# Two more tiles turned on TensorE and six more gate buffers in a recurrence-and-router kernel

## The chip, the cores and the metric

One core of one Trainium2 chip runs the whole kernel. The metric is device time in microseconds (us) from launch to end. TensorE (PE), VectorE (DVE), ScalarE (ACT), GpSimd (POOL) and SyncE (SP) each run their own instructions in order, and meet only at semaphores. SP, ACT and POOL can also issue DMAs, which move data between the chip's memory (HBM) and the on-chip buffers (SBUF).

## The reference, cut to what matters

```python
# x, f_logit: (4, 5056, 256); B*S = 20224 tokens, D = 256, E = 8 experts, F = 1024
f = lb + (1 - lb) * sigmoid(f_logit)
h[t] = f[t] * h[t-1] + (1 - f[t]) * x[t]            # per batch and channel; y[t] = h[t]
logits = normalise(y) @ normalise(emb).T / tau      # 20224 x 8
e = argmax(logits);  g = softmax(logits)[e]
out[token] = g * (relu(y[token] @ w1[e]) @ w2[e])   # one expert per token
```

## The kernel before, in words

**First half: chunks.** The tokens are taken in 40 chunks of 512 (the last has 256). For each chunk SP loads `f_logit` and `x` (`load`, three buffers each). PE transposes them so that channels lie on partitions (`F_`, `X_`), ACT makes the forget gate (L791, L797), and DVE does the recurrence as a scan along the tokens (L838). `Y_` turns the result back to token rows, in bf16, in `Yt`: early chunks by PE, from chunk 14 on by a transposing DMA that SP issues (L869). `route_` and `gate_` find each token's expert, its gate weight and its place in that expert's list. POOL then scatters each 128 rows into the HBM scratch `Xs` with an indirect DMA (L1107). A row of `Xs` is 256 bf16 values, the gate weight and the token's number: the "token and gate words" of the change.

**Second half: tiles.** As soon as an expert's list has 256 rows, they can be a tile. `update_` writes a small table that says for each tile where its rows start in `Xs` and which expert's weights it needs. `tile_(j, u, g, n)` emits tile `j` as the `n`-th in order. Its steps are:

- Load of the rows into `ys` as two 128 x 256 halves, channels on partitions. For all but the first tiles this is a transposing DMA on SP (`ld`, L1329). For the first `NPE` = 4 tiles SP issues a plain load into the output buffer `osb` instead (`ldp`, L1350), PE multiplies its four 128 x 128 blocks by the identity (`turn`, L1381), and ACT copies the result into `ys` (L1395).
- Load of the gate weight and token number of each row into `xm[n % NX]`, `NX` = 8 (`ldm`, L1339). SP issues it for 75 tiles. The six main tiles of the last table (`last`, j = 75 to 80, taken in order places n = 70, 72, 74, 76, 78 and 80) come in halves, and there ACT issues the `xm` loads.
- `mm1` on PE (L1432, 16 matmuls of 256 columns, or 32 of 128 for the last table's tiles), relu into `hT` by ACT (L1453) and DVE (L1458), `mm2` on PE (L1480, 16 matmuls).
- Scaling by the gate into `osb[n % 6]`, one half by ACT (L1495) and one by DVE (L1499). Both read `xm`.
- Two indirect DMAs on POOL that scatter 128 rows each to `out` (L1505). They read `osb`, and take the token numbers from `xm`.

So an `xm` buffer is free again only when both scatters of the tile that used it have landed: the load of tile n waits for the scatters of tile n - `NX`. In the same way `osb` is reused after 6 tiles, and `ys` after 6 (there it is `mm1` that must have read it).

**The order of the work.** A planner (`Prog.schedule`) decides before launch the order in which each engine issues its instructions. It simulates the engines with costs written in the code, and takes at each moment the ready operation of lowest priority number: chunk work first, tiles after. An operation is ready in it when the operations that it depends on have ended by its own clock. The order of each queue is then fixed, and `emit` puts in front of each instruction the waits that correctness needs. If something lands later on the chip than in the plan, its engine stands there, and everything behind it in that queue stands too. Output scatters and `Xs` scatters also wait for a step of PE that lies ahead of them in the plan (`paced`). PSUM has eight banks, which are given out in the plan by kind (`Hold`: "a" for chunk work and turns, "m" for `mm1`, "o" for `mm2`).

The lines that set the loads and their buffers:

```python
qx, qy, qh, qo = n % NX, n % NYS, n % NHT, n % NO        # L1318
op("act" if last else "sp", lambda e, s=s: ldm(e, s), ..., r=rd, w=[("xm", qx, k) ...], order=[lo])  # L1367
```

Of the kernel before, what the change touches and what calls it, by code (L numbers as in the profile page):

```python
# [370 lines left out]
def bass_hgrn_recurrence__then__cosine_router_kernel(  # L371
# [41 lines left out]
    with ExitStack() as es:  # L413

        def sb(name, shape, dt=F32):
            return es.enter_context(nc.sbuf_tensor(name, shape, dt))
# [70 lines left out]
        nullv = sb("nullv", [P, 2])  # L487
        tbl = [sb(f"tbl{q}", [P, 2], I32) for q in range(NU)]
        nrow = sb("nrow", [P, E], I32)
        NX = 8  # L490
        xm = [sb(f"xm{q}", [P, 2, 2], I32) for q in range(NX)]
        NHF = 3
        hbf = [sb(f"hbf{q}", [P, DT * CH], BF16) for q in range(NHF)]
        CT = 14
        NYS = 6
        NPE = 4
        ys = [sb(f"ys{q}", [P, T * DT], BF16) for q in range(NYS)]
        NHT = 2
        hT = [sb(f"hT{q}", [P, FT, T], BF16) for q in range(NHT)]
# [816 lines left out]
        def tile_(j, u, g, n):  # L1316

            qx, qy, qh, qo = n % NX, n % NYS, n % NHT, n % NO  # L1318
            last = u == len(ups) - 1
# [5 lines left out]
            def ld(e, s):  # L1325
                r = reg(e, f"row{j}_{s}")
                e.load(r, tbl[u][rows[s] : rows[s] + 1, 0:1])
                r = evl[j, s] = e.snap(r, donate=True, min_val=0, max_val=NULLROW)
                return e.dma_start_transpose(  # L1329
                    ys[qy][:, s * R_ * DT : (s + 1) * R_ * DT].rearrange("p (k t) -> p k t", k=DT),  # L1330
                    Xs[bass.ds(r, R_), 0:P].bitcast(BF16),
                )

            def ldm(e, s):
                if last:
# [5 lines left out]
                    Xs[bass.ds(evl[j, s], R_), P : P + 2].rearrange(  # L1341
                        "(p s) r -> p s r" if j < NPE else "(s p) r -> p s r", p=P
                    ),
# [15 lines left out]
            for s in range(halves):  # L1359
                lo = op(  # L1360
                    "sp", ldp, 950, r=rd, w=[("osb", qo, k) for k in range(2)],
                    dma=f"xs{qy}", nbytes=140000,
                ) if j < NPE else op(
                    "sp", lambda e, s=s: ld(e, s), 1750, r=rd, w=[("ys", qy, k) for k in ([s] if last else [0, 1])], dma=f"xs{qy}" + "b" * s,
# [8 lines left out]

            if j < NPE:
                hy = Hold("a")
# [255 lines left out]
```

## Time and profile before

| | us |
|---|---|
| median of three timed runs | 472.71 (471.99 to 473.21) |
| the profiled execution | 476.37 |
| its span, from the first to the last instruction | 474.6 |
| PE busy | 438.5 (92%) |
| DVE, ACT, POOL busy | 359.6, 325.6, 332.0 |
| DMA | 100.47 MB, mean 212 GB/s |

Durations of single instructions come from the profiled execution. A group of matmuls is shown as one line with its first start and its length; as they are pipelined, the distance between the starts of two groups says what a group costs PE. "Idle before" is how long an engine had stood ahead of an instruction, with the event that ended it. "issue" there means that nothing shown ended it. DMA-issuing instructions are not in the busy time of SP and ACT; POOL's indirect DMAs are, with 0.30 us of issue between any two.

### The profile page before, as it was taken

To read this page: it belongs to the slowest core of one execution; us is meant where nothing else is said; L and a number is where in the kernel's file an instruction comes from. 1 tells how busy PE (TensorE), PEld (TensorE's weight loads), DVE (VectorE), ACT (ScalarE), POOL (GpSimd) and SP (SyncE) were. 2 spreads that over 40 slices of the span, in tenths; PEclk is the share of its full clock that TensorE was granted. 3 is DMA by queue.
4 is the path that set the end of the run, shared out by engine and by line. 5 is a ranking of instruction groups with operands and counts; after the bars stand their busy time and mean duration, and the time that the engine had idled before them with its cause. 6 is when DMAs were issued, how large, how long until landed. Compare 5 with 4: busy or idle time off the path is not lost. (4 is left out here: it accounts for less than half of the span.)

```text
span 474.6 us, 12386 instructions
## 1 busy us (share of the span) xinstructions
PE 438.5 (92%) x4098; PEld 376.5 (79%) x4098; DVE 359.6 (76%) x1075; ACT 325.6 (69%) x571; POOL 332.0 (70%) x388
## 2 busy tenths in 40 slices
PE   6866868889989999999999999999999999979994
PEld 4564555669768889888888789999999999969993
DVE  6887999999998999999999997545545455345442
ACT  4877898999899899899899555444444444244441
POOL 8144657767776777777777777777777777775554
PEclk8989999999999999999999999999999999989999
DMA  7999999999999999999996644655454444553311
GB/s 235 309 308 309 309 320 324 293 286 263 279 269 301 301 305 304 313 312 283 256 287 159 142 110 133 144 136 133 120 133 131 127 109 116 150 137 101 94 62 68
DMA packets 120481, 100.47 MB, mean 212 GB/s; under 512 B 97940, under 2 KB 99487, under 8 KB 120416
## 3 DMA queue, kind: packets, MB, share of 16 engines
q1 hardware_dynamic: 102464, 59.37, 47.9%
q0 software_dynamic: 16224, 40.26, 31.3%
q8 instruction: 36, 0.59, 0.5%
q10 hardware_dynamic: 1728, 0.01, 0.2%
q14 instruction: 29, 0.24, 0.2%
HBM read 58.93 MB, written 32.93 MB: 194 GB/s over the span
## 5 line engine op out<-in xcount | busy, mean ns | idle before, releaser
L1505 POOL DMA_INDIRECT out_dram<-osb,xm x162 | 160.7, 992 | 63.2 <-issue 30.2
L1107 POOL DMA_INDIRECT XsScratch<-Yt,sli x158 | 152.3, 964 | 57.9 <-issue 25.9
L1432 PE MATMUL bank<-ys,wall 128*128 128x256 bf16 (+1 forms) x1392 | 161.5, 267 | 3.4 <-ACT hT L1453 2.8
L1480 PE MATMUL bank<-wall,hT 128*128 x1296 | 161.3, 273 | 0.2 <-issue 0.2
L1432 PEld LDWEIGHTS bank<-ys,wall 128*128 x1392 | 146.7, 145 | 7.3 <-ACT hT L1453 3.3
L1480 PEld LDWEIGHTS bank<-wall,hT 128*128 128x128 bf16 x1296 | 125.3, 98 | 19.6 <-issue 2.2
L1453 ACT ACTIVATE hT<-bank 128x512 bf16<-128x512 f32 x162 | 96.2, 596 | 38.6 <-PE bank L1432 37.0
L1458 DVE TENSOR_SCALAR hT<-bank 128x512 bf16<-128x512 f32 x162 | 110.7, 684 | 12.5 <-PE bank L1432 7.4
L1499 DVE TENSOR_SCALAR osb<-bank,xm 128x256 f32<-128x256 f32 x81 | 38.9, 480 | 83.2 <-ACT osb L1495 81.7
L838 DVE TENSOR_TENSOR_SCAN hb<-fg,hb,bank 128x512 f32<-128x512 f32 (+4 forms) x78 | 95.9, 1235 | 0.1
L1495 ACT ACTIVATE osb<-bank,xm 128x256 f32<-128x256 f32 x81 | 38.5, 476 | 71.7 <-PE bank L1480 58.0
L797 ACT ACTIVATE fg<-th,cs 128x512 f32<-128x512 f32 (+1 forms) x80 | 64.1, 814 | 2.0 <-DVE cs L625 1.0
L814 PE MATMUL bank<-ident,xin 128*128 128x128 f32 x316 | 50.0, 283 | 12.7 <-ACT fg L797 10.7
L822 DVE SCALAR_TENSOR_TENSOR bank<-fg,bank 128x512 f32<-128x512 f32 (+1 forms) x80 | 54.4, 685 | 3.4 <-PE bank L814 2.8
L814 PEld LDWEIGHTS bank<-ident,xin 128*128 128x128 f32 x316 | 36.2, 144 | 22.0 <-ACT fg L797 14.2
L791 ACT ACTIVATE th<-bank 128x512 f32<-128x512 f32 (+1 forms) x80 | 46.1, 592 | 10.8 <-PE bank L780 10.6
L780 PE MATMUL bank<-ident,fin 128*128 128x128 f32 x316 | 47.7, 279 | 3.2 <-DMA fin<-in_f_logit_dram 1.2
L780 PEld LDWEIGHTS bank<-ident,fin 128*128 128x128 f32 x316 | 37.3, 144 | 7.9 <-issue 1.7
L850 ACT ACTIVATE sq<-hb 128x1024 f32<-128x1024 f32 (+1 forms) x40 | 41.9, 1048 | 1.7 <-DVE hb L838 1.5
L943 PE MATMUL bank<-hb,eT 128*8 128x512 f32 (+1 forms) x160 | 40.8, 588 | 0.0
L947 PE MATMUL bank<-sq,onesf 128*1 128x512 f32 (+1 forms) x160 | 40.7, 586 | 0.0
L859 ACT ACTIVATE hbf<-hb 128x512 bf16<-128x512 f32 x50 | 31.3, 632 | 3.5 <-DVE hb L838 2.0
(139 smaller groups left out, 298.1 us busy)
## 6 DMA issues: line engine op xcount, KB each, us to landing
fin<-in_f_logit_dram SPq DMA_DIRECT2D x39, 512.0 KB
xin<-in_x_dram SPq DMA_DIRECT2D x39, 512.0 KB
wall<-in_moe_w_dram POOLq DMA_DIRECT2D x16, 512.0 KB, 10.4
out_dram<-osb,xm POOLq DMA_INDIRECT x162
XsScratch<-Yt,sli POOLq DMA_INDIRECT x158
ys<-XsScratch SPq DMA_TRANSPOSE x83, 2.8
xm<-XsScratch SPq DMA_DIRECT2D x75, 2.0 KB
osb<-XsScratch SPq DMA_DIRECT2D x4, 136.0 KB
```

The lines of the kernel that those rows point to most:

```text
L780: i = e.transpose(bank[h.b][:, b : nb * P : nb], fin[q][:, b, dh * P : (dh + 1) * P], ident[:],)
L791: lambda e, dh=dh, h=h: e.activation(th[dh][:, 0:n], bank[h.b][:, 0:n], AF.Tanh, scale=0.5),
L797: lambda e, dh=dh: e.activation(fg[c % 2][:, dh, 0:n], th[dh][:, 0:n], AF.Identity, bias=cs[:, dh, 0:1], scale=cs[:, dh, 1:2],),
L814: i = e.transpose(bank[h.b][:, b : nb * P : nb], xin[q][:, b, dh * P : (dh + 1) * P], ident[:],)
L822: lambda e, dh=dh, h=h: e.scalar_tensor_tensor(out=bank[h.b][:, 0:n], in0=fg[c % 2][:, dh, 0:n], scalar=1.0, in1=bank[h.b][:, 0:n], op0=AL ...
L838: lambda e, dh=dh, s0=s0, s1=s1, init=init, h=h: e.tensor_tensor_scan(hb[c % NH][:, dh, s0:s1], fg[c % 2][:, dh, s0:s1], bank[h.b][:, s0:s ...
L1107: lambda e, j=o + j, i=o + k_ * 4 + b: e.indirect_dma_start(out=Xs[:, :], out_offset=bass.IndirectOffsetOnAxis(ap=sli[y][:, j : j + 1], axis=0
L1432: i = e.matmul(bank[hh[f // 2].b][:, at : at + R_], wall[:, bass.ds(a1[j, s][(4 * mp + f) * DT + kt] - WA - WREV, 2 * FT * P),].bitcast(BF ...
L1453: lambda e, o=o, h=h: e.activation(o, bank[h.b][:], AF.Relu), 512,
L1458: lambda e, o=o, h=h: e.tensor_scalar(o, bank[h.b][:], 0.0, None, op0=ALU.max),
L1480: i = e.matmul(po(s), hT[qh][:, kf, s * P : (s + 1) * P], wall[:, bass.ds(a2[j, s if last else 0][kf] - WA, 2 * D)].bitcast(BF16), start=( ...
L1505: lambda e, s=s: e.indirect_dma_start(out=out[:, :], out_offset=bass.IndirectOffsetOnAxis(ap=xm[qx][:, s, 1:2], axis=0), in_=osb[qo][:, s, :],
```

## The change: two numbers

The tiles j = 0 to 5 now take the plain load, the turn on PE and the ACT copy; before, j = 0 to 3 did. In `ldm` the row order that goes with the plain load holds for them too. The `xm` buffers are 14 instead of 8. Nothing else is edited; the planner makes its order anew from these numbers.

```diff
-        NX = 8
+        NX = 14
         xm = [sb(f"xm{q}", [P, 2, 2], I32) for q in range(NX)]
...
-        NPE = 4
+        NPE = 6
```

## Rows read from the trace of the kernel before

**Rows 1.** The page's parts 1 and 2: busy time; busy tenths in 40 slices.
```profile
PE 438.5 (92%) x4098; PEld 376.5 (79%) x4098; DVE 359.6 (76%) x1075; ACT 325.6 (69%) x571; POOL 332.0 (70%) x388
...
PE   6866868889989999999999999999999999979994
```

**Rows 2.** Windows of 12 us: stretch, length, busy us (count) by engine, clock, DMA.
```profile
84.00:96.00 12.00, 10.04 (x90) 7.30 (x90) 11.59 (x32) 11.97 (x20) 9.56 (x11) 1.00 1.08 304
96.00:108.00 12.00, 11.62 (x119) 9.46 (x120) 10.95 (x42) 11.17 (x22) 7.76 (x9) 1.00 1.14 282
108.00:120.00 12.00, 11.94 (x117) 10.36 (x118) 11.26 (x34) 11.47 (x21) 9.20 (x10) 1.00 1.10 265
120.00:132.00 12.00, 11.56 (x114) 10.05 (x107) 11.37 (x37) 10.08 (x19) 9.25 (x10) 1.00 1.10 286
132.00:144.00 12.00, 10.74 (x94) 8.12 (x92) 11.09 (x30) 11.12 (x20) 8.62 (x10) 1.00 1.25 258
144.00:156.00 12.00, 12.00 (x127) 10.01 (x126) 11.18 (x45) 10.83 (x19) 8.61 (x10) 1.00 1.10 281
...
396.00:408.00 12.00, 12.00 (x112) 11.34 (x111) 5.57 (x10) 5.34 (x11) 9.26 (x10) 1.00 0.44 119
```

**Rows 3.** Windows of 2 us around 418 us, same columns.
```profile
416.00:418.00 2.00, 0.00 (x0) 0.00 (x0) 0.31 (x1) 0.82 (x2) 1.59 (x2) 1.00 0.63 153
418.00:420.00 2.00, 1.80 (x9) 1.42 (x10) 1.74 (x4) 1.48 (x4) 1.39 (x3) 0.50 0.38 109
420.00:422.00 2.00, 2.00 (x14) 1.48 (x13) 0.80 (x2) 0.60 (x1) 1.70 (x2) 0.64 0.75 197
```

**Rows 4.** Timeline of PE, the `mm1` groups there: start, us, instruction, idle before.
```profile
411.08 1.91 PE L1432 MATMUL bank<-ys,wall 128*128 128x256 bf16 x16
...
414.58 1.04 PE L1432 MATMUL bank<-ys,wall 128*128 128x256 bf16 x8
418.20 1.92 PE L1432 MATMUL bank<-ys,wall 128*128 128x256 bf16 x8 [2.59 <-ACT hT L1453]
...
422.41 1.91 PE L1432 MATMUL bank<-ys,wall 128*128 128x256 bf16 x16
```

**Rows 5.** Timeline of ACT and its DMA queue (ACTq) in the same stretch.
```profile
409.54 0.60 ACT L1453 ACTIVATE hT<-bank 128x512 bf16<-128x512 f32 x1 [0.28 <-PE bank L1432]
415.73 1.33 ACTq L1339 DMA_DIRECT2D xm<-XsScratch  x2
417.18 0.47 ACT L1495 ACTIVATE osb<-bank,xm 128x256 f32<-128x256 f32 x1 [7.05 <-issue]
```

**Rows 6.** Timeline of POOL: last scatter to `Xs`; output scatter 37th from the end.
```profile
399.34 0.96 POOL L1107 DMA_INDIRECT XsScratch<-Yt,sli  x1 [0.30 <-PE bank L1432]
...
412.23 0.99 POOL L1505 DMA_INDIRECT out_dram<-osb,xm  x1 [0.30 <-PE bank L1432]
```

**Rows 7.** Waits of SP: engine, line, waited for; us in total, times, longest.
```profile
SPq L348 <- DMA out_dram<-osb,xm: 29.9, 23, 3.1
```

**Rows 8.** Timeline of SP: a plain tile load; first two transposing ones (tiles 4, 5).
```profile
85.09 0.35 SPq L1350 DMA_DIRECT2D osb<-XsScratch  x1
...
95.33 4.27 SPq L1329 DMA_TRANSPOSE ys<-XsScratch  x1
...
101.28 1.74 SPq L1329 DMA_TRANSPOSE ys<-XsScratch  x1
```

**Rows 9.** Timeline of PE: tile 1's turn, what follows, and tile 4's `mm1`.
```profile
96.31 0.40 PE L1381 MATMUL bank<-identb,osb 128*128 128x128 bf16 x4 [1.20 <-DMA osb<-XsScratch]
96.54 0.51 PE L965 MATMUL bank<-ident,lgS 98*128 98x98 f32 x4
...
123.60 1.04 PE L1432 MATMUL bank<-ys,wall 128*128 128x256 bf16 x8
```

**Rows 10.** Waits of PE: the turns' own.
```profile
PE bank L1381 <- DMA osb<-XsScratch: 1.2, 1, 1.2
```

**Rows 11.** Groups by line: ACT's copies of the turned tiles (count, busy us, mean ns).
```profile
L1395 ACT ACTIVATE ys<-bank 128x512 bf16<-128x512 f32 x4 | 2.4, 610 | 0.7 <-PE bank L1381 0.7
```

## The prediction

> **What bounds the kernel now.** I read the page's first two parts, then windows, then the timelines of the places where TensorE (PE) has holes. PE is busy 438.5 of 474.6 us, more than any other engine, and its 40 slices show where the rest lies [rows 1]: the first nine slices (to about 107 us), then 9s, one 7 near 415 us, and the end. The windows sharpen it: PE stands 1.96 us in 84 to 96, and 0.38, 0.06, 0.44 and 1.26 us in the next four windows (12.00 less the busy time), 2.14 together; from 144 us on it has 12.00 of 12.00, and so to 408 us (the first and the last of these windows stand in [rows 2]; one between them lacks 0.48). So PE sets the end: work added to it costs its length unless it falls into one of these holes, and only a closed hole gives time back.
>
> The hole near 415 us is the one that the change touches. Two `mm1` groups start at 411.08 and 414.58, which is 3.50 us for one tile; the next whole one starts at 422.41, 7.83 us after [rows 4]. One tile took 4.33 us too long. Of these 2.59 us are idle PE, put down to ACT's relu [rows 4]. The rest is clock: the granted clock is 1.00, but after 416 to 418, in which PE does nothing, it is 0.50 (1.2 GHz) in one window and 0.64 in the next [rows 3]; at half speed 1.80 busy us cost 0.90, and 0.36 of 2.00 us costs 0.72. With 2.59 that is 4.21, the same to 0.1 us.
>
> ACT is late because it stands in its own queue. It ends a relu at 409.54 + 0.60 = 410.14, and its next instructions are two `xm` loads that go out at 415.73; the gate scaling behind them had waited 7.05 us for nothing shown but "issue" [rows 5]. That 5.59 us is a semaphore wait. Which one? These are the halves of tile j = 75, at place n = 70, the first whose `xm` load ACT issues. With eight buffers it must wait for the scatters of place 62. The last place is 80, two scatters each, so the second scatter of place 62 is the 37th from the end: issued 412.23, done on POOL at 413.22 [rows 6]. ACT's load follows 2.51 us later, what a scatter would need to land. Place 62's rows had been scaled long before: its `mm1` is four tiles, some 14 us, ahead of place 66's at 407.6 (one tile before the row at 411.08). POOL lags PE, and its distance reaches back over eight buffers.
>
> **The change part by part.** *Fourteen `xm` buffers.* The load of place 70 now waits for place 56, six tiles earlier: twelve output scatters, and the last two to `Xs`, which stand between. At 1.29 us each (0.99 and 0.30 of issue [rows 6]) that is 18.1 us, so it has landed near 415.73 - 18.1 = 397.6, before ACT comes to the load at 410.14. The ACT stall of 5.59 us goes, and with it PE's 4.33 us. What is late next? Three things. The same load also needs all rows in `Xs`: the last such scatter ends at 399.34 + 0.96 = 400.30 [rows 6], with 2.51 us to land 402.8. The plan can't put the load much before that, as it comes after the row load of its tile, whose `ys` buffer is freed by the `mm1` of place 64 (two tiles before 411.08, at 404.1). The `osb` buffers, six, would be the next limit: place 68's scaling needs the scatters of place 62, landed at 415.73, and falls without the stall at about 418. That holds with 2 us to spare and more later, since a tile costs POOL 2.58 us and PE 3.50. The third is PE itself, which is full again. I take -4.33; bounds -4.33 and 0.
>
> SP loses its waits for output scatters, 29.9 us in 23 waits [rows 7]. They cost PE nothing now, as it is full while SP stands (these waits lie after 250 us, where its only hole but 0.48 us is this one), so their end gives nothing: 0, on either side.
>
> *Tiles 4 and 5 turned on PE.* Removed: two transposing loads, whose issue holds SP for 4.27 and 1.74 us [rows 8]. Added: two plain loads of 0.35 us each on SP, eight matmuls, two ACT copies. The next PE group begins 0.23 us after a turn [rows 9], so two turns are 0.46 us, in windows that are full but for 2.14 us [rows 2]; I count them whole: +0.46, bounds 0 and +0.80 (two times the 0.40 us length).
>
> The Trainium skill, "TensorE: Matmul & The Clock Gate", Part 4 (PE-mode transpose), gives about 275 ns for one 128 x 128 bf16 transpose inside a kernel. As an estimate by that page the eight would be 2.2 us, and the sum below would be -1.5 instead of -3.3. Here a block is an ordinary matmul against the identity, and the row has four of them in 0.23 us; the row decides.
>
> A turn adds a wait on PE, and behind it stands all of PE's queue: the chunks' transposes, which feed ACT and DVE, and the tiles. Of the four turns now one waited, tile 1's, 1.20 us [rows 9, 10]: its plain load was issued at 85.09 and PE could start at 96.31, 11.2 us after [rows 8, 9], in a stretch where the DMA engines are full (share above 1 in every window [rows 2]). Two more turns: between 0 and 2.40 us; I take the mean of the four, 0.30 each: +0.60.
>
> The two ACT copies are 0.61 us each [rows 11], 1.22 us where ACT is busy 11.17 and 11.47 of 12 [rows 2]. It has 1.36 us free in these two windows, so I take 0; without that cover up to +1.22, as PE's transposes of `x` wait for the gate that ACT makes.
>
> What SP gains, 4.27 + 1.74 - 0.70 = 5.31 us, lets the next chunk loads go out earlier, and a plain load may move through the DMA engines faster than a transposing one. Tile 4's own data is in no hurry: it was asked for at 95.33 and first used at 123.60 [rows 8, 9]. PE's holes there are all that this can give: between 0 and -2.14 [rows 2]. I take 0, since PE's order is fixed and the holes have several causes. The planner makes a new order from the two numbers; that can open or close holes of the size seen in 120 to 144, 0.44 to 1.26 us [rows 2]. I cost it at 0, with 1.3 us either way.
>
> The sum: -4.33 + 0.46 + 0.60 = -3.27. The profiled execution took 476.37 us (span 474.6 and 1.8 around it), so it would be 473.1; the median of the timed runs is 3.66 us lower, and I put the same step on it: 472.71 - 3.27 = 469.4.
>
> **The rivals.** *The hole is mostly the profiler's.* The timed runs are 3.66 us shorter than the profiled one. PE has nothing to give between 144 and 414 us, so the difference comes from the start, the hole or the end. POOL issues scatters without a pause, so if it is slightly quicker in a timed run, place 62's scatter lands in time. If all 3.66 are the hole, only 0.67 is left to win and 1.06 of turns is added: 473.1, no change. For it: the size fits; 320 scatters would make up the 5.59 us at 0.017 us each. Against: the first 107 us hold far more idle time in which an execution can differ. Chance 0.20.
>
> *The wait moves to another event of POOL.* With the buffer free, the plan puts ACT's load earlier, where it waits for the last `Xs` scatter, landing at 402.8, or the scaling waits for `osb`. POOL's lag is the same, and ACT again stands several us. Then 472.71 + 1.06 = 473.8, no change. For it: POOL was 5.59 us later than the plan put it. Against: the row load comes first in the plan, and the 2 us to spare on `osb`. Chance 0.08.
>
> *The turns stall PE, slower.* If the plan puts the two new turns as near to their loads as tile 1's, and these take longer to land in the fuller stretch (1.14 against 1.08 [rows 2]), PE stands in a stretch whose order is fixed. From 3.3 us in the two together the gain of the hole is gone, from 4.7 it is slower by more than can be told. Five us beyond the 0.46, two of tile 1's waits in each turn, give 472.71 - 4.33 + 0.46 + 4.8 = 473.6; the same beside a hole that the timed runs hardly have (0.67) gives 472.71 - 0.67 + 0.46 + 4.8 = 477.3. For it: one of four waited. Against: the other three did not make PE wait, and chunk work fills PE meanwhile. With the planner's new order in a worse shape as its second way to the same end, chance 0.12.
>
> **How the numbers follow.** My forecast, -3.27 with its bounds, has 0.60: 469.4, by itself 466.7 (no waits at the turns, 1.3 from the order, some of the holes) to 471.3. Up to the first two rivals the range reaches 474.0; above it lies most of the slower case, and together with what is below 466.7 I leave out some 0.17. What a measurement can tell from no change is 0.3%, 1.4 us: faster is below 471.3. The forecast case gives 0.58 of that and a hole that is half the profiler's 0.05, so 0.63; the same 0.21; slower 0.16.
>
> **What would show it.** Right: ACT's two `xm` loads near place 70 go out without a gap ahead of them; PE's `mm1` groups stay 3.50 us apart through 405 to 425 us, with the clock at 1.00; six turns of about 0.23 us, the waits for plain loads under 2.4 us together; windows full from 144 us on as before. Wrong: an ACT gap of several us in the same place with another scatter landing at its end; a new PE hole behind a turn between 96 and 125 us; or a trace that shows the hole closed while the timed median stays within 1.4 us.

## The result and the profile after

The changed kernel takes 470.18 us (median of six runs, 468.62 to 471.86); the kernel of before 474.18 (median of six: the three of the table of before, and three later ones at 475.15 to 476.47). The ratio is 0.9893, 95% interval 0.9859 to 0.9926. In a second set of runs it was 0.9871 (0.984 to 0.9901, e5 below). The ratios leave out executions more than 1.5% above the fastest of their kernel; the medians in us leave out none. The profiled execution took 471.86 us, of which 470.0 are the span.

First the page's parts 1 and 2 of the changed kernel, as in [rows 1]. PE's slices from the ninth to the last but one are all 9; the 7 near 415 us is gone.

```profile
PE 439.7 (94%) x4106; PEld 376.4 (80%) x4106; DVE 359.0 (76%) x1075; ACT 328.1 (70%) x573; POOL 331.9 (71%) x388
...
PE   7865878899999999999999999999999999999994
```

The windows of the changed kernel, to be read against [rows 2] and [rows 3]. PE lacks 0.14 and 0.17 us in the two windows from 96 to 120 and nothing in 120 to 144; in these four it lacked 2.14 us before. From 396 to 432 it is full, with the clock at 1.00.

```profile
84.00:96.00 12.00, 9.85 (x92) 7.17 (x91) 11.67 (x36) 11.91 (x20) 9.47 (x11) 1.00 1.06 286
96.00:108.00 12.00, 11.86 (x119) 9.27 (x120) 11.36 (x40) 11.89 (x23) 8.14 (x9) 1.00 1.11 355
108.00:120.00 12.00, 11.83 (x122) 10.36 (x124) 11.76 (x34) 11.45 (x21) 9.26 (x10) 1.00 1.13 228
120.00:132.00 12.00, 12.00 (x124) 10.80 (x113) 11.98 (x43) 11.81 (x23) 8.94 (x11) 1.00 1.11 299
132.00:144.00 12.00, 12.00 (x111) 9.97 (x110) 11.20 (x30) 11.58 (x21) 9.25 (x10) 1.00 1.16 280
...
396.00:408.00 12.00, 12.00 (x113) 11.39 (x111) 6.06 (x11) 6.08 (x11) 9.19 (x10) 1.00 0.45 124
408.00:420.00 12.00, 12.00 (x113) 11.39 (x111) 6.34 (x11) 5.84 (x11) 9.02 (x10) 1.00 0.62 138
420.00:432.00 12.00, 12.00 (x140) 11.25 (x138) 6.10 (x11) 5.38 (x10) 9.25 (x10) 1.00 0.66 142
```

ACT's timeline there, against [rows 5]: the two gate loads of place 70 go out at 404.58 and 405.48, between other work, with no gap of ACT ahead of them that PE would not have caused.

```profile
403.95 0.47 ACT L1495 ACTIVATE osb<-bank,xm 128x256 f32<-128x256 f32 x1 [1.20 <-PE bank L1480]
404.58 0.40 ACTq L1339 DMA_DIRECT2D xm<-XsScratch  x1
405.02 0.60 ACT L1453 ACTIVATE hT<-bank 128x512 bf16<-128x512 f32 x1 [0.60 <-PE bank L1432]
405.48 0.34 ACTq L1339 DMA_DIRECT2D xm<-XsScratch  x1
```

POOL's output scatters, against [rows 6]: the 49th from the end (place 56, which the load must now wait for) and the 37th (place 62, which it would have waited for with eight buffers). The first is done on POOL at 395.06, 9.5 us before the load; the second is issued 7.5 us after it.

```profile
394.07 0.99 POOL L1505 DMA_INDIRECT out_dram<-osb,xm  x1 [0.30 <-issue]
...
412.10 0.98 POOL L1505 DMA_INDIRECT out_dram<-osb,xm  x1 [0.30 <-issue]
```

PE's two new turns and what follows them, against [rows 9]: the next group starts 0.22 us after each, and none waits. No turn is in the list of PE's waits any more [rows 10].

```profile
110.81 0.39 PE L1381 MATMUL bank<-identb,osb 128*128 128x128 bf16 x4
111.03 0.61 PE L814 MATMUL bank<-ident,xin 128*128 128x128 f32 x4
111.48 0.39 PE L1381 MATMUL bank<-identb,osb 128*128 128x128 bf16 x4
111.70 0.61 PE L780 MATMUL bank<-ident,fin 128*128 128x128 f32 x4
```

SP's timeline, against [rows 8]: the plain loads of tiles 4 and 5, then a chunk's transposing DMA. The first is issued in 0.35 us, the second holds SP for 3.91, the third for 4.36 (2.61 in the kernel before).

```profile
94.77 0.35 SPq L1350 DMA_DIRECT2D osb<-XsScratch  x1
...
96.35 3.91 SPq L1350 DMA_DIRECT2D osb<-XsScratch  x1
...
102.50 4.36 SPq L869 DMA_TRANSPOSE Yt<-hbf  x1
```

### The profile page after: what moved, and what is told of

Its sections match the earlier page's. It is cut to its first block, busy times and chain, and to the rows that moved or that the text cites. A ratio compares the mean times of both kernels' runs of the same rounds, so it can differ in the third digit from the quotient of the medians.

```text
span 470.0 us, 12406 instructions
## 1 busy us (share of the span) xinstructions
PE 439.7 (94%) x4106; PEld 376.4 (80%) x4106; DVE 359.0 (76%) x1075; ACT 328.1 (70%) x573; POOL 331.9 (71%) x388
## 5 line engine op out<-in xcount | busy, mean ns | idle before, releaser
L1480 PE MATMUL bank<-wall,hT 128*128 x1296 | 166.3, 273 | 0.6 <-DVE nr L555 0.3
L1432 PE MATMUL bank<-ys,wall 128*128 128x256 bf16 (+1 forms) x1392 | 165.1, 267 | 0.0
L780 PE MATMUL bank<-ident,fin 128*128 128x128 f32 x316 | 49.4, 284 | 3.5 <-DMA fin<-in_f_logit_dram 1.9
```

Source lines behind the costliest of these rows:

```text
L780: i = e.transpose(bank[h.b][:, b : nb * P : nb], fin[q][:, b, dh * P : (dh + 1) * P], ident[:],)
L1432: i = e.matmul(bank[hh[f // 2].b][:, at : at + R_], wall[:, bass.ds(a1[j, s][(4 * mp + f) * DT + kt] - WA - WREV, 2 * FT * P),].bitcast(BF ...
L1480: i = e.matmul(po(s), hT[qh][:, kf, s * P : (s + 1) * P], wall[:, bass.ds(a2[j, s if last else 0][kf] - WA, 2 * D)].bitcast(BF16), start=( ...
```

## The experiments

Theory A is the prediction's: ACT's gate loads wait for a late output scatter, and that wait alone makes the hole. Theory B: the gain is the planner's new order or the turned tiles. Theory C: the hole is mostly the profiler's. All times are medians; ratios are to the kernel of before on the same chip. e1 to e4 ran on one chip, e5 to e8 on a second, e9 to e12 on a third.

| | buffers, turned tiles | us | before | ratio (95%) |
|---|---|---|---|---|
| e1 | 14, 4, order of before | 472.33 | 476.48 | 0.9933 (0.9901 to 0.9964) |
| e2 | 9, 4, order of before | 471.97 | 476.48 | 0.9919 (0.9887 to 0.9951) |
| e3 | 14, 4 | 472.52 | 476.48 | 0.9926 (0.9896 to 0.9955) |
| e4 | 8, 6 | 473.89 | 476.48 | 0.9952 (0.9922 to 0.9982) |
| e5 | 14, 6 (the change) | 470.47 | 476.31 | 0.9871 (0.984 to 0.9901) |
| e6 | 14, 4, as e3 | 473.05 | 476.31 | 0.9931 (0.9901 to 0.996) |
| e7 | 14, 8 | 471.14 | 476.31 | 0.9886 (0.9851 to 0.992) |
| e8 | 14, 0 | 473.98 | 476.31 | 0.9936 (0.9899 to 0.9972) |
| e9 | 14, 4, 90 ns | 568.74 | 572.33 | 0.9941 (0.9904 to 0.9978) |
| e10 | 14, 6, 90 ns | 569.52 | 572.33 | 1.0046 (0.9989 to 1.0102) |
| e11 | 14, 4, 110 ns | 566.69 | 572.33 | 0.9925 (0.9887 to 0.9963) |
| e12 | 14, 6, 110 ns | 569.96 | 572.33 | 0.9972 (0.9939 to 1.0004) |

**e1: 14 buffers in the order of before.** The planner is given extra edges, from the users of place n - 8 to the gate load of place n, which no engine waits for on the chip. Every engine issues in exactly the order of before.

```diff
-        NX = 8
+        NX = 14
...
-            left[id(o)] = len(o.deps) + len(o.order)
-            for d in o.deps:
+            left[id(o)] = len(o.deps) + len(o.order) + len(o.plan)
+            for d in o.deps + o.plan:
...
+            old, lms = used.pop(n % 8, []), []
...
+                lms.append(lm); lm.plan = old
...
+                sc.paced = n < NM - 4; used.setdefault(n % 8, [ua, ud] + lms).append(sc)
```

> 14 gate buffers, but the planner is made to count 8, so that every engine issues in the order of before; only what a gate load waits for on the chip differs. Theory A (ACT's gate loads wait for a late output scatter, and that alone makes the hole near 415 us): no hole, the two gate loads near 410 us go out without a gap, time 4.3 us under before (3.5 to 4.8). Theory B (the gain is in the planner's new order or in the turned tiles): at most 1 us under before. Theory C (the hole is mostly the profiler's): hole closed in the trace, time within 1.4 us of before.

Measured: 0.67% under before, 3.2 us (1.7 to 4.7). ACT's timeline in e1: same instruction order as in [rows 5], and the two loads follow the relu without a gap.

```profile
409.56 0.60 ACT L1453 ACTIVATE hT<-bank 128x512 bf16<-128x512 f32 x1 [0.28 <-PE bank L1432]
410.10 1.20 ACTq L1339 DMA_DIRECT2D xm<-XsScratch  x2
411.42 0.48 ACT L1495 ACTIVATE osb<-bank,xm 128x256 f32<-128x256 f32 x1 [1.26 <-PE bank L1480]
```

POOL in e1, the 37th output scatter from the end: place 62's second comes as late as before, but nobody waits for it.

```profile
412.48 0.99 POOL L1505 DMA_INDIRECT out_dram<-osb,xm  x1 [0.30 <-PE bank L1432]
```

PE in e1: the `mm1` groups run on 3.49 to 3.50 us apart where [rows 4] has 7.83.

```profile
411.11 1.91 PE L1432 MATMUL bank<-ys,wall 128*128 128x256 bf16 x16
...
414.60 1.91 PE L1432 MATMUL bank<-ys,wall 128*128 128x256 bf16 x16
...
418.10 1.91 PE L1432 MATMUL bank<-ys,wall 128*128 128x256 bf16 x16
```

So the wait for the buffer makes the hole, not the order and not the turned tiles. Theory C falls too: the timed runs gain. They gain 3.2 where the trace's hole was 4.33; the interval holds both, so a hole somewhat smaller in the timed runs than in the trace is not excluded.

**e2: the same with 9 buffers.** The edit of e1 with `NX = 9`.

> As e1, with 9 real buffers. Theory A: ACT's load of place 70 waits for the scatters of place 61, two scatters (2.58 us) earlier than place 62's; the 5.59 us gap on ACT shrinks to about 3.0, which is what PE can bear (5.59 - 2.59), so PE's idle time there is 0 to 0.5 us, the clock stays at 1.00, and the time is 3.8 to 4.3 us under before. Theory B: nothing. If the stall depends on the buffers but not on the scatter, the gap stays 5.6 us.

Measured: 0.81% under before, 3.9 us. The load moves as theory A says. In ACT's timeline the relu ends at 407.70 and the loads go out at 410.62, a gap of 2.92 us (expected 3.0):

```profile
407.10 0.60 ACT L1453 ACTIVATE hT<-bank 128x512 bf16<-128x512 f32 x1 [0.28 <-PE bank L1432]
410.62 1.20 ACTq L1339 DMA_DIRECT2D xm<-XsScratch  x2
411.95 0.48 ACT L1495 ACTIVATE osb<-bank,xm 128x256 f32<-128x256 f32 x1 [4.26 <-issue]
```

In POOL's, the 39th output scatter from the end, place 61's second, is done at 408.45, 2.17 us before the loads:

```profile
407.46 0.99 POOL L1505 DMA_INDIRECT out_dram<-osb,xm  x1 [0.30 <-issue]
```

PE did not stand at all (4.00 busy in each 4 us from 408 to 424). PE bore a gap of 2.92 us on ACT without standing, as 5.59 - 2.59 had said, and one more buffer was enough. SP still waits for output scatters in this trace, 12.9 us in 16 waits, where e1's has none; the two kernels gain alike, so these waits of SP cost nothing to be seen.

**e3 and e6: only the 14 buffers.** The first edit of the change without the second, in two sets of runs.

> Only the 14 buffers, four turned tiles, planner's own order. Theory A: 4.3 us under before, give or take 1.3 for the new order; hole gone. Theory B with the turned tiles as the cause: 0 to 1 us. The changed kernel against this one then gives the turned tiles' part: my forecast for it was +1.06 us, so this one should be 0.5 to 1 us faster than the changed kernel (about 5 us under before).

> Only the 14 buffers, as e3, for the comparison with e5 on the same chip: about 0.8% under before.

Measured: 0.74% and 0.69% under before, like e1: the planner's other order is worth nothing to be seen here. But the expected half to one microsecond under the changed kernel did not come. These kernels are over it, by 0.33% (0.9926 against 0.9893, in two sets of runs) and by 0.60% (0.9931 against 0.9871, in one set): 1.6 and 2.9 us.

**e4: only the six turned tiles.** The second edit without the first.

> Only the six turned tiles, 8 buffers. Theory A: the hole near 415 us stays (ACT gap of several us ahead of the first gate loads on its queue), and the time is 0 to 1.1 us over before. Theory B: 3 to 4 us under before, without the hole.

Half as theory A has it. The hole stays: in ACT's timeline the relu ends at 411.63, the loads go out 5.84 us later, and the next relu had waited 7.09.

```profile
411.03 0.60 ACT L1453 ACTIVATE hT<-bank 128x512 bf16<-128x512 f32 x1 [0.28 <-PE bank L1432]
417.47 1.20 ACTq L1339 DMA_DIRECT2D xm<-XsScratch  x2
418.71 0.60 ACT L1453 ACTIVATE hT<-bank 128x512 bf16<-128x512 f32 x1 [7.09 <-issue]
```

PE stood 2.26 us for it; `mm1` and `mm2` lie in another order here, and the clock stayed at 1.00. PE's timeline, then the window of 2 us in which the wait ends:

```profile
419.37 1.05 PE L1480 MATMUL bank<-wall,hT 128*128 x8 [2.26 <-ACT hT L1453]
```
```profile
418.00:420.00 2.00, 0.63 (x6) 0.58 (x7) 0.29 (x1) 1.28 (x3) 1.25 (x2) 1.00 0.52 118
```

Yet the time is 0.48% under before, 2.3 us (0.9 to 3.7), not over. A hole 2.1 us cheaper than before's 4.33 would be nearly all of that in this one trace; how large it is in the timed runs is not known.

**e5, e7, e8: six, eight and no turned tiles with 14 buffers,** run beside e6; only `NPE` differs.

> The changed kernel beside the kernel of before, more rounds, on one chip with e6 to e8: about 1.0% under before. Against e6 (only the 14 buffers): if two more turned tiles cost PE their 0.46 us and a wait now and then, 0.5 to 1 us over e6; if they help (a transposing load's long issue kept SP from the chunk loads), under e6 by 0.5 to 2 us.

> 14 buffers, eight turned tiles. If a turned tile costs: 0.5 to 1 us over e5 (0.23 us of PE and 0.61 of ACT each, and two plain loads that must wait for the output scatters of tiles 0 and 1, whose buffers they take). If it helps: under e5.

> 14 buffers, no turned tile: the first four tiles too take transposing loads. If a turned tile costs: 0.5 to 2 us under e6. If turned tiles help because a transposing load issued early stands for some 4 us on SP (95.33 in the trace of before) and lands late: 1 to 4 us over e6, with PE waiting for rows between 84 and 110 us.

Six and eight lie at 0.9871 and 0.9886, none and four at 0.9936 and 0.9931. Six are faster than four by more than was expected of them (2.9 us by the ratios, where 0.5 to 2 was the most), and none turned is level with four. Eight against six is not decided: the 0.7 us between their medians lies within the noise, and both expectations fit it. In e8's trace the waits for rows between 84 and 110 us that were to make it slower are not there. The rival in which turns stall PE does exist, though. PE in e7's trace stood 4.39 us ahead of its second turn, for one plain load:

```profile
99.13 0.61 PE L1381 MATMUL bank<-identb,osb 128*128 128x128 bf16 x4 [4.39 <-DMA osb<-XsScratch]
```

That execution took 476.04 us, the longest of e7's six; the median of the six is 471.14.

**e9 to e12: other orders.** The planner's allowance for a signal (`PAD`) is 90 or 110 ns instead of 100, with four and with six turned tiles, to see whether six win in any order.

```diff
-    PAD = 100
+    PAD = 90
```

> 14 buffers, four turned tiles; the planner allows 90 ns instead of 100 for a signal between engines, which changes nothing that is computed, only the order. If the six turned tiles help by themselves (some 2 us less than four, whatever the order), this is 2 us over e10. If what e5 won over e6 is one order's luck, the difference between e9 and e10 takes either sign, as that between e11 and e12.

> As e9 with six turned tiles: 2 us under e9 if the turned tiles help by themselves, either sign if it is the order.

> As e9 with 110 ns: a third order for four turned tiles. If the order alone matters by 1 to 3 us, the three kernels with four turned tiles (e6, e9, e11) lie that far apart from one another.

> As e11 with six turned tiles: 2 us under e11 if the turned tiles help by themselves, either sign if it is the order.

Here four beat six in both orders, by 0.8 and 3.3 us in the medians; by the ratios it is 0.9941 against 1.0046 and 0.9925 against 0.9972. (e10's median lies under that of before while its ratio lies over 1, so little hangs on this ratio.) The three kernels with four turned tiles, e6, e9 and e11, have ratios within 0.16% of one another, 0.8 us at 476; the medians of e9 and e11 lie 2.1 us apart. Whether the order alone matters by 1 to 3 us, these three neither show nor exclude. But these four ran on a third chip, on which the kernel of before takes 572.33 us. PE is busy 83 to 84% there, and is not full after 144 us as it is on the others. PE's timeline in e9 has single matmuls of one `mm1` some 0.7 us apart, with nothing shown that they wait for:

```profile
379.84 0.31 PE L1432 MATMUL bank<-ys,wall 128*128 128x256 bf16 x1 [1.09 <-issue]
...
380.58 0.27 PE L1432 MATMUL bank<-ys,wall 128*128 128x256 bf16 x1 [0.42 <-issue]
...
381.31 0.87 PE L1432 MATMUL bank<-ys,wall 128*128 128x256 bf16 x6 [0.46 <-issue]
```

So the question was put where PE is not full, and whether the answer carries over is not shown. It stays open whether six turned tiles help by themselves or by the order that the planner made of them.

## Why the prediction was right, and where it was not

**Right: the hole, its cause and that nothing took its place.** The forecast was 469.4 with a fall of 3.27 us; measured is 470.18 and a fall of 4.0 between the medians, by the ratio 5.1 (3.5 to 6.7). That the time came out within 0.8 us is in part luck. The hole gave 0.4 to 1.1 us less than its term; the rest of the change came out 2.7 to 4.0 us better than its +1.06 (below); and the base of 472.71, three runs, was low: the same kernel took 474.18 over six runs, and 476.48 and 476.31 in the later sets. The chain of the argument, from PE's idle time to ACT's relu, to ACT's own queue, to the scatters of place 62, is shown by e1, which takes away the waits for gate buffers and leaves every engine's order as it was, and by e2, where one buffer more moves the loads to a scatter two earlier. Neither the last `Xs` scatter nor `osb` made a new wait: PE is full from 396 to 432 us. (One reading on the way was off by a tile: the `mm1` at 404.1 is that of place 65, and place 64's starts at 400.60. Nothing hung on it, as the loads went out at 404.58 and 405.48.) Of the term of -4.33 the timed runs with the buffers alone give 3.2 to 3.9 us in four measurements, each with an interval of about 1.5 us to either side.

**Right: SP's own waits for output scatters cost nothing.** They were 29.9 us and are gone from SP's list, and e1 with the same order gained no more than the hole was worth. SP now stands for the `ys` buffers instead, 28.2 us against 9.9 before.

**Wrong by its sign where PE is full: the two turned tiles.** The step that failed is their +1.06 us (+0.46 for the turns, +0.60 for waits). Six against four came out at -1.6 us (changed kernel and e3), -2.9 (e5 and e6) and -2.3 (e4 and before, with a hole that differs). The intervals of the first pair overlap, and those of the second just touch; on the third chip, where PE is not full, the sign is the other one. The turns themselves were sized well, 0.22 us each against 0.23; the waits were 0 in this profile, where 0.60 was allowed.

What may outweigh them is among the terms that I set at 0: PE's holes between 96 and 144 us, with bounds 0 and -2.14, and the new order, 1.3 either way. The long windows of the changed kernel, first its first trace, then e5's, lack 0.71 and 1.38 us from 96 to 264 us:

```profile
96.00:144.00 48.00, 47.69 (x462) 40.40 (x463) 46.30 (x144) 46.72 (x84) 35.59 (x37) 1.00 1.13 291
144.00:264.00 120.00, 119.60 (x1148) 98.94 (x1147) 116.49 (x365) 109.67 (x193) 91.02 (x94) 1.00 1.12 274
```
```profile
96.00:144.00 48.00, 47.68 (x462) 40.44 (x463) 46.27 (x144) 46.91 (x85) 35.50 (x38) 1.00 1.11 287
144.00:264.00 120.00, 118.94 (x1139) 98.06 (x1137) 115.92 (x358) 109.38 (x193) 90.79 (x94) 1.00 1.11 276
```

The same stretch lacks 2.59 us in e3, and in e6, with only the buffers, 2.77:

```profile
96.00:144.00 48.00, 46.71 (x448) 39.01 (x447) 45.38 (x142) 43.94 (x78) 35.46 (x37) 1.00 1.15 270
144.00:264.00 120.00, 118.52 (x1132) 97.86 (x1129) 115.81 (x351) 108.96 (x194) 90.50 (x93) 1.00 1.09 279
```

That is 1.2 to 2.1 us in the right direction. It is no proof: e4, with six turned, lacks 3.55 us there, e2, with four, 1.42, and one execution of a kernel says little of such holes (below). The cause of this part is not settled.

**Wrong in its reason: what SP gains.** I counted 5.31 us of SP's time won, as if the 4.27 and 1.74 us of issue belonged to the transposing form. In the changed kernel a plain load stands 3.91 us in the same place, and the DMA behind it 4.36 instead of 2.61: 6.01 + 2.61 = 8.62 us before, 0.35 + 3.91 + 4.36 = 8.62 after. In these three issues SP won nothing.

**The rivals.** That the hole is mostly the profiler's is refuted by e1's time. The 3.66 us that spoke for it were those of three timed runs: beside the 476.37 of the profiled execution, later medians of the same kernel are 476.48 and 476.31. The wait that moves to another event of POOL did not come at 14 buffers; e2 shows it at 9, small enough to be free. The stalling turn was seen once, 4.39 us in e7's trace, and not in the changed kernel's. The bounds that I gave for this rival, 3.3 and 4.7 us, hold only on top of the 0.60 already in the sum. Counted whole they are 3.87 and 5.3 us, and the rival's own 4.8 us of waits, 473.6, would have been no change that can be told.

## What to carry to other kernels

A DMA that an engine issues from between its compute instructions can hold up that engine's line, as it held ACT for 5.59 us here: look for a gap of ACT or DVE put down to "issue" just behind a DMA issue, count back which earlier transfer freed the buffer, and compare how far the releasing engine lags, here some 14 us of POOL against eight buffers (place 62's rows were scaled by 398.4 us, its second scatter was issued at 412.23 [rows 6]). One more buffer was enough here (e2), and five beyond it showed no cost in time (e1), so give small buffers the depth of the slowest consumer. Where a planner makes the order anew, hold the order fixed, as e1 does, before the gain is put down to a wait; and in a kernel whose second part differs by some 2 us, believe no single trace for it.

## What the runs showed of the hardware that was not expected

- How long a DMA takes to issue on SP did not go by its form. In the changed kernel's trace two plain 136 KB loads, issued within 2 us of one another, took 0.35 and 3.91 us, while the DMA engines were full (share 1.06 and 1.11 in their windows).
- The clock: after PE had stood idle for 2.59 us the granted clock was 0.50 in the next window [rows 3, 4]; with 2.26 us idle in e4 it stayed at 1.00. Behind the 4.39 us of e7 it was 0.50 from 98 to 102 us, so that wait cost more than its own length.
- Two kernels with the same order on every engine, e1 and e2 on one chip, have spans of 470.4 and 467.8 us in their traces. In 96 to 144 us PE lacks 2.74 us in the one and 0.94 in the other. The code that differs between them, the waits for gate buffers, shows no wait in either trace before 250 us.
- Between chips the same kernel of before takes 476 and 572 us. In e9's trace on the slow one single instructions have nearly the lengths that they have in the trace of before (the scan 1235 ns in both, `mm1`'s matmuls 272 and 267); what is longer is the time between them. PE idles 93.6 us of e9's span and 36.1 of before's. Why is not known.
